# Conversions' products moved to VectorE, batch 1 masked by TensorE, batch 2 in cluster order, and a staggered order of quarter products in a fused routing-attention and PReLU-FFN kernel

## The chip, the cores and the metric

The kernel runs on one core of a Trainium2 chip. The metric is the time on the device in microseconds (us), median of three runs. Engines are named as the profile names them: PE is TensorE's matmuls and PEld its weight loads, DVE is VectorE, ACT is ScalarE, POOL is GpSimd, SP is the engine that issues most DMAs.

## What is computed

Attention over 4 batches, 8 heads, 768 tokens of 64 elements, in which a query sees only the keys that fall to the same one of 16 clusters, and behind it a feed-forward block (512 to 2048 to 512) with a leaky slope for each hidden element. The weights come as float64.

```python
q_assign = np.argmax(np.einsum('bhsd,hcd->bhsc', q_n, c_n), axis=-1)
k_assign = np.argmax(np.einsum('bhsd,hcd->bhsc', k_n, c_n), axis=-1)
mask = q_assign[:, :, :, None] == k_assign[:, :, None, :]
scores = scale * np.matmul(q, k.transpose(0, 1, 3, 2))
scores = np.where(mask, scores, -1000000000.0)
attn = softmax(scores)                 # written out in the source
x = (attn @ v).transpose(0, 2, 1, 3).reshape(B * S, H * D)
h = x @ w_in
out = (np.maximum(h, 0.0) + alpha * np.minimum(h, 0.0)) @ w_out
```

## The kernel before

**Units.** A pair `n` is one batch and two heads; there are 16 pairs, four a batch. `WHOLE = 3` batches (pairs 0 to 11, `NO = 12`) are computed against all keys: for each half of the queries (384 of them), six chunks of 128 keys for two heads. The last batch (pairs 12 to 15) is computed in cluster order: its tokens are sorted by cluster first, so that a chunk of keys meets only a window of two or three blocks of queries (L755). float32 matmuls appear in the trace as two instructions each.

**Steps.** `steps` (L747) is a list written out by hand: six steps for a pair of the whole kind (two halves of three), three for a pair in cluster order; 84 in all. Every piece of side work is put at a step and slot (`prep_at`, `load_at`, L1203 to L1247) or so many slots later (`later`, L93). Each engine executes its own instructions in the order in which the program issues them; SP's queue of DMAs too, and a DMA that waits holds all DMAs behind it on SP.

**First part** (steps 0 to 23, batch 0, the loop at L1280). The masks of batch 0 are made by TensorE: the clusters as one-hot rows (`member`, `outside`, L449 to L468; `prep_queries`, L496) go into a second, bfloat16 matmul that adds a large negative number where the clusters differ (`early_mask`, L779 and L796 to L803). The float64 weights are converted meanwhile, 32 tiles of 128 by 512 (`convert`, L241): DVE takes the words apart (`split`, L250 and L252), ACT scales (L256, L258), DVE joins (L262, L265) and POOL multiplies (L268). For the first weight matrix, four tiles make a group of quarters, from which POOL forms four sums (L305 to L313); the eight forms go to DRAM (`put`). This is an FFN by Strassen's scheme: seven products where a plain one takes eight.

**Second part** (L1321). At the first step of a half (s == 0) come the whole half's scores, in between the weighted sums (`weigh`) of the half before; then 12 slots, in which the pieces of the FFN of the batch before are fed so that they last (`feed_down_to`). Batches 1 and 2 are masked on DVE (`mask`, L822: one instruction for each chunk and head, L833, with keys from `prep_clusters`, `prep_keys`). A pair in cluster order is sorted beforehand (`order_features` to `order_scatter`): 6 stages, each of three loads on SP (L687) into one of two buffers and four scatters on POOL (L698), queued in `sorting`, of which one item is taken per slot; `order_load` fetches the sorted pair three to four steps before its start; afterwards `normalise_near`, `to_rows`, `put_back` (12 scatters on POOL, L998) and `fetch_back` bring the result back into token order.

**The FFN's hidden part** (`hidden`, L1084) makes seven products for each x, in PSUM banks a, z and b; ACT copies (five per x), DVE adds (three per x, L1077) and applies the slopes (two per x, L1081). The forms come by two loads per x into double buffers (`fetch_sums`, L1042). `final` (L1136) does the second matrix (L1147).

Of the kernel before, what the change touches and what calls it, by code (L numbers as in the profile page):

```python
# [23 lines left out]
def kernel(  # L24
# [22 lines left out]
    WHOLE = 3  # L47
# [11 lines left out]
    inp = fast.enter_context(tc.tile_pool(name="inp", bufs=4))  # L59
    vpool = fast.enter_context(tc.tile_pool(name="vpool", bufs=3))  # L60
    qkp = fast.enter_context(tc.tile_pool(name="qkp", bufs=2))
    fsp = fast.enter_context(tc.tile_pool(name="fsp", bufs=4))
# [6 lines left out]
    wsum = fast.enter_context(tc.tile_pool(name="wsum", bufs=2))  # L69
# [5 lines left out]
    memp = first_part.enter_context(tc.tile_pool(name="memp", bufs=2))  # L75
    raws = first_part.enter_context(tc.tile_pool(name="raws", bufs=1))
    cvt = first_part.enter_context(tc.tile_pool(name="cvt", bufs=3))
# [163 lines left out]
    def convert(src, dst, then):  # L241
# [6 lines left out]
        def split():  # L248
            power.append(cvt.tile([P, CW], U32, name="power"))
            nc.vector.tensor_scalar(out=power[0], in0=hi, scalar1=0x7FF00000, scalar2=None,  # L250
                                    op0=ALU.bitwise_and)
            nc.vector.tensor_scalar(out=dst.bitcast(U32), in0=hi, scalar1=0x000FFFFF,  # L252
                                    scalar2=None, op0=ALU.bitwise_and)
# [7 lines left out]
        def join():  # L261
# [6 lines left out]
            nc.gpsimd.tensor_tensor(out=dst, in0=dst, in1=power[0].bitcast(FP32),  # L268
# [23 lines left out]
    def quarters(x0, cc):  # L292
# [9 lines left out]
        def add():  # L302
# [4 lines left out]
            def summed(to, a, b, op):  # L307
                nc.gpsimd.tensor_tensor(out=forms[:, to, :], in0=forms[:, a, :],
                                        in1=forms[:, b, :], op=op)
            summed(S1, A21, A22, ALU.add)  # L310
            summed(S2, S1, A11, ALU.subtract)
            summed(S3, A11, A21, ALU.subtract)
            summed(S4, A12, S2, ALU.subtract)  # L313
# [22 lines left out]
    begun, converted = [0], [0]  # L336

    def fetch(ahead):

        while ((sources or coming) and len(fetched) < ahead  # L340
               and begun[0] + len(fetched) - converted[0] < len(raw_tiles)):
            fetched.append(convert(*next_source()))

    def advance(stages):
        stages.pop(0)()
        if stages:
            later(4 if len(stages) == 2 else 2, lambda: stages and advance(stages))
# [101 lines left out]
    def prep_argmax(n, ps):  # L449
        top, first, pieces = argmax(ps, exact=n < NCH)  # L450
# [3 lines left out]
        if n >= NCH:  # L454
# [41 lines left out]
    def prep_queries(n, half, h):  # L496
# [3 lines left out]
        if n < NCH:  # L500
# [25 lines left out]

    def second_part():

        first_part.close()
        for name, bufs in (("gpool", NQ), ("ypool", NJ), ("ppool", 2), ("emore", 1),  # L530
                           ("ordc", 1), ("ordp", 1), ("order", NP - NO), ("byrow", 1)):
            sorts[name] = fast.enter_context(tc.tile_pool(name=name, bufs=bufs))
        for i in range(4):
            e_tiles.insert(0, sorts["emore"].tile([P, 2, HS], FP32, name=f"more{i}"))

# [77 lines left out]
    def order_counts(n, ps):  # L613
# [6 lines left out]
        def scan():  # L620
            count = asg.tile([P, HS], FP32, name="simT")
# [3 lines left out]
        for i, piece in enumerate(pieces):  # L625

            later(i if i < len(pieces) - 2 else i + 2, piece) if i else piece()

# [18 lines left out]
    def order_rows(n, begin, count):  # L647
# [17 lines left out]
        later(2, lambda: order_clusters(n, begin))  # L665
# [107 lines left out]
    def score(n, half, chunks, alone=None):  # L773
# [5 lines left out]
        early_mask = n < NCH  # L779
# [42 lines left out]
    def mask(chunk):  # L822
        n, half, c, E = chunk
        if n < NCH:
# [210 lines left out]
    lagging, coming_sums = deque(), {}  # L1035
    MM, MM2 = KH * HS, DM

# [4 lines left out]
    def fetch_sums(i):  # L1042

        if i >= B * NQ:
            return
        parts = []
        for name, m0, m1 in (("early", 0, FORMS_A), ("late", FORMS_A, A21)):
            t = wsum.tile([P, m1 - m0, KH, P], FP32, name=name)
            nc.sync.dma_start(out=t, in_=by_form[i % NQ, :, m0:m1])
            parts.append(t)  # L1050
        coming_sums[i] = parts

    def ffn_pieces(b):
        rows = out[b * S:(b + 1) * S, :].rearrange(
            "(p j) n -> p j n" if b == 0 else "(j p) n -> p j n", p=P)
        gs, ys, banks, parts = {}, {}, {}, {}
# [12 lines left out]
        def product(x, k, m, rhs, start):  # L1069
            w = parts[x][m >= FORMS_A][:, m % FORMS_A]  # L1070
            for cc in range(KH):
                nc.tensor.matmul(out=bank(k), lhsT=w[:, cc, :], rhs=rhs[:, cc, :],  # L1072
                                 start=start and cc == 0, stop=cc == KH - 1,
                                 skip_group_check=not start)

# [8 lines left out]
        def hidden(x):  # L1084

            f1, f2 = x, NQ + x

            def first():
                flush()
                parts[x] = coming_sums.pop(b * NQ + x)  # L1090
                for f in (f1, f2):
                    gs[f] = sorts["gpool"].tile([P, 2, HS], FP32, name="gT")
                product(x, "a", A11, B11, True)
                nc.scalar.copy(gs[f1][:, 0, :], bank("a"))

            def second():
                product(x, "z", A12, B21, True)
                z = bank("z")
                banks.pop("z")
                lagging.append(lambda: plus(gs[f1][:, 0, :], z))  # L1100

            def third():
                product(x, "a", S2, T2, False)
                flush()
                nc.scalar.copy(gs[f1][:, 1, :], bank("a"))  # L1105

            def fourth():
                product(x, "b", S1, T1, True)
                parts["p5"] = sorts["ppool"].tile([P, HS], FP32, name="p5")
                nc.scalar.copy(parts["p5"], bank("b"))  # L1110

            def fifth():
                product(x, "a", S3, T3, False)
                nc.scalar.copy(gs[f2][:, 1, :], bank("a"))  # L1114
                p5 = parts.pop("p5")
                lagging.append(lambda: plus(gs[f2][:, 1, :], p5))

            def sixth():
                product(x, "b", S4, B22, False)
                flush()  # L1120
                end = bank("b")
                banks.pop("b")
# [500 lines left out]
```

## Time and profile before

| | |
|---|---|
| median of 3 runs | 1024.39 us (1024.2 to 1024.44) |
| the profiled execution | 1021.29 us, of it 1019.5 us span from the first to the last instruction |
| PE busy | 960.2 us, 94% of the span, 4019 matmul instructions |
| DVE busy | 692.3 us, 68% |
| ACT busy | 277.9 us, 27% |
| POOL busy | 235.5 us, 23% |
| DMA | 98.24 MB, 95 GB/s of HBM traffic over the span |
| first FFN product (L1072) | begins at 174.7 us |

A line of a window gives its length, then each engine's busy time in it with the number of instructions in brackets, in the order PE, PEld, DVE, ACT, POOL, then the granted TensorE clock (1.00 is full), the share of the DMA engines' time and GB/s. A line of the timeline gives the start, the length, the engine, the source line, the operation, what it writes and reads, the shapes, how many instructions are merged, and in brackets for how long the engine was idle before and what released it. A line of groups gives the count, the total busy time and the mean in ns of one instruction, then the engine's idle time just before.

### The profile page before, as it was taken

The numbers are of one execution on the slowest core, as the hardware profiler recorded it, in microseconds if no ns is written. First come the engines' busy times: TensorE is split into PE (matmuls) and PEld (weight loads), VectorE is DVE, ScalarE is ACT, GpSimd is POOL, SyncE is SP. The second block draws the span as 40 slices with busy tenths as digits, with TensorE's granted clock in tenths as the row PEclk, the third lists the DMA queues.
The fourth block names the chain that finished last, engine by engine and source line by source line (L and its number), as shares of the span: only waits on it lengthen the run. The fifth ranks groups of instructions, "written<-read, shape, count | busy, mean of one in ns | idle before, by whom it ended". The sixth has DMA issues, their size and how long they took to land.

```text
span 1019.5 us, 11293 instructions
## 1 busy us (share of the span) xinstructions
PE 960.2 (94%) x4019; PEld 469.4 (46%) x4019; DVE 692.3 (68%) x1178; ACT 277.9 (27%) x499; POOL 235.5 (23%) x265
## 2 busy tenths in 40 slices
PE   7976978899998899998999999999999999999997
PEld 4432433454444544444344554455445544544544
DVE  3899999987767986878878677777556624310320
ACT  4655555231232211232122331113113200201200
POOL 1464533100051323301633330000431430000000
PEclk8978988999999999998999999999999999999999
DMA  5397874362315338273520333442402322200101
GB/s 200 119 283 232 223 211 93 94 111 49 62 49 111 94 72 137 72 128 90 111 63 21 109 106 71 78 94 93 94 10 76 107 59 71 102 23 20 53 31 34
DMA packets 200544, 98.24 MB, mean 96 GB/s; under 512 B 162768, under 2 KB 182944, under 8 KB 200480
## 3 DMA queue, kind: packets, MB, share of 16 engines
q1 hardware_dynamic: 194880, 89.05, 35.4%
q0 software_dynamic: 4608, 7.87, 2.3%
q8 instruction: 34, 0.56, 0.2%
q10 hardware_dynamic: 992, 0.52, 0.2%
q14 instruction: 30, 0.25, 0.1%
HBM read 74.51 MB, written 22.54 MB: 95 GB/s over the span
## 4 chain that ended last, share of the span: by engine, by line
PE 75%; DVE 21%; issue 2%; ACT 1%; POOL 0%; ACTq 0%; DVEq 0%; POOLq 0%
PE fps L1147 30%; PE fps L1072 23%; PE fps L928 7%; PE sps L792 6%; PE fps L792 3%; DVE power L262 2%; DVE acc L843 2%; DVE more L833 2%; DVE power L250 1%; DVE forms L252 1%; DVE gT L1081 1%; DVE w_out_sb L265 1%; DVE forms L265 1%; DVE w_out_sb L252 1%; DVE gT L1077 1%
## 5 line engine op out<-in xcount | busy, mean ns | idle before, releaser
L1147 PE MATMUL fps<-w_out_sb,gT 128*128 128x512 f32 x752 | 331.5, 596 | 2.0 <-DVE gT L1081 2.0
L1147 PEld LDWEIGHTS fps<-w_out_sb,gT 128*128 128x128 f32 x752 | 140.1, 190 | 174.4 <-issue 166.0
L1072 PE MATMUL fps<-xT,early 128*128 128x384 f32 x512 | 177.6, 497 | 1.4 <-DVE gT L1077 1.0
L698 POOL DMA_INDIRECT scratch<-stage,off x96 | 101.5, 1058 | 302.9 <-DMA stage<-in_v_dram 106.3
L1072 PE MATMUL fps<-xT,late 128*128 128x384 f32 x384 | 133.1, 495 | 0.0
L1072 PEld LDWEIGHTS fps<-xT,early 128*128 128x128 f32 x512 | 96.7, 193 | 71.7 <-issue 7.7
L792 PE MATMUL sps<-qkT 64*128 64x384 f32 (+1 forms) x516 | 105.9, 532 | 4.4 <-ACT more L813 3.5
L1072 PEld LDWEIGHTS fps<-xT,late 128*128 128x128 f32 x384 | 73.8, 194 | 50.5 <-issue 3.4
L998 POOL DMA_INDIRECT back<-rows,place x48 | 47.5, 989 | 184.6 <-ACT rows L993 171.5
L1077 DVE TENSOR_TENSOR gT<-gT,fps 128x384 f32<-128x384 f32 x64 | 35.1, 548 | 68.0 <-PE fps L1072 68.0
L833 DVE SCALAR_TENSOR_TENSOR E<-aq,key,E 128x384 f32<-128x384 bf16 (+1 forms) x120 | 66.1, 606 | 18.6 <-ACT E L810 11.0
L928 PE MATMUL fps<-E,vt 128*64 128x384 f32 x384 | 75.2, 518 | 3.1 <-DVE xT L1029 3.1
L813 ACT ACTIVATE E<-sps 128x768 f32<-128x768 f32 (+1 forms) x87 | 65.4, 802 | 44.3 <-PE sps L801 37.7
L833 DVE SCALAR_TENSOR_TENSOR more<-aq,key,more 128x384 f32<-128x384 bf16 (+1 forms) x120 | 65.8, 604 | 12.8 <-ACT more L813 6.4
L792 PEld LDWEIGHTS sps<-qkT 64*128 64x128 f32 x516 | 49.4, 200 | 51.4 <-issue 16.0
L1158 DVE TENSOR_TENSOR y<-y,fps 128x512 f32<-128x512 f32 x23 | 15.8, 687 | 80.2 <-PE fps L1147 80.2
L1081 DVE SCALAR_TENSOR_TENSOR gT<-gT,alpha 128x768 f32<-128x768 f32 x64 | 62.9, 1013 | 2.2 <-ACT gT L1128 1.7
L1077 DVE TENSOR_TENSOR gT<-gT,p 128x384 f32<-128x384 f32 x32 | 17.7, 554 | 62.0 <-ACT gT L1114 62.0
L1156 ACT COPY y<-fps 128x512 f32<-128x512 f32 x24 | 14.1, 586 | 155.0 <-PE fps L1147 155.0
L928 PEld LDWEIGHTS fps<-E,vt 128*64 128x64 f32 x384 | 24.9, 142 | 42.1 <-issue 35.7
L813 ACT ACTIVATE more<-sps 128x768 f32<-128x768 f32 (+1 forms) x42 | 31.3, 795 | 43.9 <-PE sps L792 29.8
L1105 ACT COPY gT<-fps 128x384 f32<-128x384 f32 x32 | 15.3, 479 | 78.1 <-PE fps L1072 78.1
(193 smaller groups left out, 982.6 us busy)
## 6 DMA issues: line engine op xcount, KB each, us to landing
early<-sums SPq DMA_DIRECT2D x32, 512.0 KB, 3.7
late<-sums SPq DMA_DIRECT2D x32, 384.0 KB, 3.4
raw<-in_moe_w_in_dram SPq DMA_DIRECT2D x16, 512.0 KB, 6.3
sums<-forms SPq DMA_DIRECT2D x32, 256.0 KB, 4.5
raw<-in_moe_w_out_dram SPq DMA_DIRECT2D x16, 512.0 KB, 4.4
out_dram<-y SPq DMA_DIRECT2D x23, 256.0 KB, 2.1
vt<-in_v_dram SPq DMA_DIRECT2D x12, 384.0 KB, 5.4
qk<-in_q_dram SPq DMA_DIRECT2D x48, 96.0 KB, 3.8
```

Of the source, the lines that this page charges most:

```text
L252: nc.vector.tensor_scalar(out=dst.bitcast(U32), in0=hi, scalar1=0x000FFFFF, scalar2=None, op0=ALU.bitwise_and)
L262: nc.vector.scalar_tensor_tensor(out=power[0], in0=hi, scalar=0x80000000, in1=power[0], op0=ALU.bitwise_and, op1=ALU.bitwise_or)
L698: nc.gpsimd.indirect_dma_start(out=scratch[n][1][h * NX + xx], out_offset=bass.IndirectOffsetOnAxis(ap=ranks[n][:, xx, h:h + 1], axis=0), ...
L792: nc.tensor.matmul(out=bank(ps, h, m), lhsT=qkT[r:r + D, S + c * P:S + (c + 1) * P], rhs=qkT[r:r + D, tokens], start=True, stop=not early_ ...
L813: nc.scalar.activation(out=E[:, :, 0:m], in_=ps[:, :, 0:m], func=AF.Exp, scale=SCALE)
L833: nc.vector.scalar_tensor_tensor(out=e, in0=of, scalar=keys[n][:, NJ + c, h:h + 1], in1=e, op0=ALU.is_equal, op1=ALU.mult)
L928: nc.tensor.matmul(out=po[r:r + D, 0:HS], lhsT=vts[n][:, h, c, :], rhs=e[:, h, :], start=(c == 0), stop=(c == NJ - 1))
L998: nc.gpsimd.indirect_dma_start(out=to[i], out_offset=bass.IndirectOffsetOnAxis(ap=place[:, h, j:j + 1], axis=0), in_=rows[:, j, h * D:(h + ...
L1072: nc.tensor.matmul(out=bank(k), lhsT=w[:, cc, :], rhs=rhs[:, cc, :], start=start and cc == 0, stop=cc == KH - 1, skip_group_check=not start)
L1077: nc.vector.tensor_tensor(out=to, in0=to, in1=of, op=ALU.add)
L1081: nc.vector.scalar_tensor_tensor(out=g, in0=g, scalar=alpha[:, f:f + 1], in1=g, op0=ALU.mult, op1=ALU.max)
L1147: nc.tensor.matmul(out=ps[:, 0:DM], lhsT=gs[f][:, half, t * P:(t + 1) * P], rhs=w_out_sb[:, f, :], start=on and f == fs[0], stop=off and f ...
```

## The change

Five things at once, in one diff:

1. **Conversions.** The product that ends a conversion and the four sums of quarters go from POOL to DVE; the sums are spread over later slots. Only 24 of 32 conversions are done in the first part, one a step; eight come in the second part, two to each half of batch 1, with one raw buffer instead of five.
2. **Batch 1 masked by TensorE.** The conditions `n < NCH` become `n < NO`, so pairs 4 to 7 are masked by bfloat16 matmuls like batch 0, and the DVE masks, keys and query transposes of these pairs go. Rows of clusters come by DMAs on ACT's queue, as in batch 0.
3. **Batch 2 in cluster order.** `WHOLE = 2`: pairs 8 to 15 are sorted; 72 steps instead of 84. Sorting begins at steps 24, 27, 30, 33, 39, 42, 45 and 48, and two queued items are taken per slot.
4. **Quarter products.** The seven products of an x come in another order, the fourth (p4) held over into the next x; the first product is copied within PSUM by ACT so that the second accumulates onto it; DVE adds two instead of three per x. Forms are fetched one by one, eight ahead.
5. **Order at a half's start.** The weighted sum of two chunks comes before the new scores; two exp buffers fewer. The FFN of batch 1 lasts until step 66, that of batch 2 begins there, and 14 pieces of it (11 before) are kept for the time after the last step.

The diff, cut to its core:

```diff
-    WHOLE = 3
+    WHOLE = 2
-    inp = fast.enter_context(tc.tile_pool(name="inp", bufs=4))
+    inp = fast.enter_context(tc.tile_pool(name="inp", bufs=6))
-    wsum = fast.enter_context(tc.tile_pool(name="wsum", bufs=2))
+    wsum = fast.enter_context(tc.tile_pool(name="wsum", bufs=8))
...
-            nc.gpsimd.tensor_tensor(out=dst, in0=dst, in1=power[0].bitcast(FP32),
+            nc.vector.tensor_tensor(out=dst, in0=dst, in1=power[0].bitcast(FP32),
                                     op=ALU.mult)
...
             def summed(to, a, b, op):
-                nc.gpsimd.tensor_tensor(out=forms[:, to, :], in0=forms[:, a, :],
+                nc.vector.tensor_tensor(out=forms[:, to, :], in0=forms[:, a, :],
                                         in1=forms[:, b, :], op=op)
-            summed(S1, A21, A22, ALU.add)
-            summed(S2, S1, A11, ALU.subtract)
-            summed(S3, A11, A21, ALU.subtract)
-            summed(S4, A12, S2, ALU.subtract)
+            later(1, lambda: summed(S1, A21, A22, ALU.add))
+            later(1, lambda: summed(S2, S1, A11, ALU.subtract))
+            later(2, lambda: summed(S3, A11, A21, ALU.subtract))
+            later(2, lambda: summed(S4, A12, S2, ALU.subtract))
...
+    limit = [W_IN + 2 * FQ]
...
+               and begun[0] + len(fetched) < limit[0]
...
     def prep_argmax(n, ps):
-        top, first, pieces = argmax(ps, exact=n < NCH)
+        top, first, pieces = argmax(ps, exact=n < NO)
...
-        if n >= NCH:
+        if n >= NO:
             return
...
-        early_mask = n < NCH
+        early_mask = n < NO
...
     def mask(chunk):
         n, half, c, E = chunk
-        if n < NCH:
+        if n < NO:
             return
...
-        for i in range(4):
+        for i in range(2):
             e_tiles.insert(0, sorts["emore"].tile([P, 2, HS], FP32, name=f"more{i}"))
+        fast.enter_context(middle)
+        cvt[0] = middle.enter_context(tc.tile_pool(name="cvt2", bufs=1))
+        raw2 = middle.enter_context(tc.tile_pool(name="raws2", bufs=1))
+        raw_tiles[:] = [raw2.tile([P, CW, 2], U32, name="raw5")]
+        limit[0], first_ends[0] = W_IN + NF, now[0]
...
+    ORDER_OF_FORMS = (A11, S2, A12, S1, S3, S4, A22)
+    wanted = deque((b, x, m) for b in range(B) for x in range(NQ) for m in ORDER_OF_FORMS)
+    def fetch_sums(n):
+        for _ in range(n):
+            if wanted:
+                b, x, m = wanted.popleft()
+                t = wsum.tile([P, KH, P], FP32, name="form")
+                nc.sync.dma_start(out=t, in_=by_form[x, :, m])
+                coming_sums[b, x, m] = t
...
+            def product(k, m, rhs, start):
+                w = coming_sums.pop((b, x, m))
+                for cc in range(KH):
+                    nc.tensor.matmul(out=bank(k), lhsT=w[:, cc, :], rhs=rhs[:, cc, :],
+                                     start=start and cc == 0, stop=cc == KH - 1,
+                                     skip_group_check=not start)
+                fetch_sums(1)
+            def p1():
                 flush()
...
+                product(a, A11, B11, True)
+                nc.scalar.copy(bank(z), bank(a))
+                order = [p6, p2, p5] if pending else [p5, p6, p2]
+                rest.extend(order)
+                settle()
+            def p2():
+                product(z, A12, B21, False)
+                nc.scalar.copy(gs[f1][:, 0, :], bank(z))
+                banks.pop(z)
...
+            def p3():
+                product(e, S4, B22, False)
                 flush()
+                of = bank(e)
+                banks.pop(e)
+                lagging.append(lambda: plus(gs[f1][:, 1, :], of))
+                pending.append(p4)
...
-    ORDERS = [28, 34, 46, 52]
+    ORDERS = [24, 27, 30, 33, 39, 42, 45, 48]
...
-    KEPT = {B - 2: 11 * MM2 * FQ}
+    SHORT, LONG = 2 * MM2 * FQ, 14 * MM2 * FQ
+    STAGES_OF_FFN = {TOGETHER: (0, SHORT), NO * 2 * SB: (1, LONG),
+                     (NO * 2 + NCH) * SB: (None, SHORT), (NO * 2 + NCH + 2) * SB: (2, LONG),
+                     NS: None}
...
-            if u >= 0 and i < CONVERTING[u % len(CONVERTING)]:
+            if u >= 0 and i == 0:
                 convert_next()
...
             tick()
+            near = prior[1] is None
+            invert(prior[0], *((0, 1) if near else prior[1:])) if u > TOGETHER else None
+            if near:
+                weigh_near(0)
+            else:
+                weigh(GROUP, denominators=u == TOGETHER)
             if u < NS:
                 score(n, half, range(0, GROUP))
...
-            if sorting:
+            for _ in range(min(2, len(sorting))):
                 sorting.popleft()()
+            if (s, i) in ((1, 0), (2, 2)):
+                convert_next()
```

## The prediction, made before the changed kernel ran

> **What bounds the kernel now.** I read the page's slices first, then windows that cut the span at the two joints I could place in the timeline: 173 us (just before the first FFN product) and 418 us (batch 1's last half); 696 us, where the first pair in cluster order is weighed.
>
> ```profile
> PE   7976978899998899998999999999999999999997
> DVE  3899999987767986878878677777556624310320
> ```
> ```profile
> 0.00:173.00 173.00, 140.76 (x1149) 64.89 (x1149) 147.84 (x256) 93.56 (x143) 74.86 (x89) 0.88 0.70 200
> 173.00:418.00 245.00, 233.21 (x871) 109.78 (x871) 200.28 (x341) 59.82 (x114) 51.38 (x65) 0.98 0.41 86
> 418.00:696.00 278.00, 271.41 (x996) 131.98 (x992) 218.57 (x364) 69.25 (x134) 61.75 (x64) 0.99 0.38 87
> ```
>
> Two regimes. In the first 173 us PE has holes and a clock of 0.88, while DVE is full: 140.0 of the 155 us from 18 to 173. From 173 us on PE is busy 95 to 98% at a clock near 1; there only less PE work, or the 18 us of PE's waits (11.9 before 418 us, 6.5 to 696 us, all on DVE), can shorten the time.
>
> The second view is DVE and POOL side by side in the first part, where every conversion ends on POOL.
>
> ```profile
> 77.83 0.42 DVE L250 TENSOR_SCALAR power<-raw 128x512 uint32<-128x512 uint32 x1
> 78.17 0.42 DVE L252 TENSOR_SCALAR forms<-raw 128x512 uint32<-128x512 uint32 x1
> 78.50 0.69 DVE L262 SCALAR_TENSOR_TENSOR power<-raw,power 128x512 uint32<-128x512 uint32 x1
> 79.10 0.69 DVE L265 SCALAR_TENSOR_TENSOR forms<-raw,forms 128x512 f32<-128x512 uint32 x1
> ...
> 85.17 1.49 DVE L252 TENSOR_SCALAR forms<-raw 128x512 uint32<-128x512 uint32 x1
> 86.58 1.77 DVE L262 SCALAR_TENSOR_TENSOR power<-raw,power 128x512 uint32<-128x512 uint32 x1
> 88.28 1.75 DVE L265 SCALAR_TENSOR_TENSOR forms<-raw,forms 128x512 f32<-128x512 uint32 x1
> ```
> ```profile
> 86.34 6.22 POOL L308 TENSOR_TENSOR forms<-forms 128x512 f32<-128x512 f32 x4
> ```
>
> The same four instructions take 0.42, 0.42, 0.69, 0.69 us while POOL is idle, and 1.5 to 1.8 us while it adds or multiplies. So POOL does not relieve DVE here; it makes it pay.
>
> **First part: what changes.** Today's five DVE groups (L262 30.4, L250 19.5, L252 18.5 and 13.2, L265 16.3 and 14.2) sum to 112.1 us for 32 conversions, 3.50 each. Without POOL one costs 0.42 + 0.42 + 0.69 + 0.69, and the product that moves to DVE. For that I have no row of the same shape from SBUF to SBUF; L843 (two float32 SBUF inputs) takes 949 ns for 768 columns, L1077 548 for 384, so 512 lie at 0.69 us. One conversion: 2.91 us; 24 make 69.8, 16 sums of quarters 11.0, together 80.9. DVE sheds 31 us of the 140 and has 109 left after 18 us. PE is next: a step's work from back-to-back starts is 1.50 (L792), 0.42 (L801), 0.79 (L921) and 1.44 (L928), 4.15 us; 23 steps after 18 us make 95.5, features of three pairs 3 x 2.75 and four clusters' products 4 x 0.78 bring it to 107. Two engines at 107 and 109 us can't both run full in order. The steps before DVE filled up (18.12 to 44.80 us, five of them) had 24.3 us of PE work in 26.7, 91%; the bursts at each half's end (transposes, reciprocals, L1029) and the argmax stay, so I take 88%: 122 us, end at 140 instead of about 168 (the start of step 24's scores). Gain **27 us**; bounds 43 (PE never waits, end at 125) and 0 (the four DVE instructions stay at 3.50 us: 24 x 4.19 + 11 = 112, nothing shed). ACT (about 83 us after eight conversions go) and DMA (0.70 of 173 us, four MB less) fit under 122.
>
> **Batch 1.** TensorE's mask costs 0.42 us for four bfloat16 matmuls, 24 times: **+10.1 us** of PE, on the path. Their cluster rows come by four small DMAs a pair on ACT's queue; a copy or exp behind one waits with it, but the rows are made some four steps ahead and ACT is busy 60 of 245 us here. DVE loses 96 masks of 0.616 (59 us), 16 transposes L512 (9) and keys (2); it gains eight conversions (23), and the ordering of about four more pairs at 9.9 each (two L599 of 0.97 and fifteen small ones from L437 to L677, 8.0 in sum): 40. Fewer plain preparations (-7), sharper argmax (+3) and an add less per x (-4) leave about 185 us where 200 were. Eight late conversions lie in slots under FFN products, and the second matrix needs their tiles only from about step 42, some five steps after the last; without that cover they would cost PE at most their 23 us.
>
> **Batch 2.** A half's block of scores and sums against all keys, and a whole pair in cluster order:
>
> ```profile
> 226.48 1.56 PE L792 MATMUL sps<-qkT 64*128 64x384 f32 x8
> ...
> 235.12 0.85 PE L416 MATMUL mps<-qkT,cT 128*32 128x384 f32 x8
> ```
> ```profile
> 735.71 1.35 PE L792 MATMUL sps<-qkT 64*128 64x256 f32 x8
> ...
> 743.51 1.98 PE L1147 MATMUL fps<-w_out_sb,gT 128*128 128x512 f32 x4
> ```
>
> 8.64 us twice against 7.80 once: 9.48 less per pair. It pays six transposes back to rows (L990, 24 in 3.9 us: 0.98) and two beginnings (0.36 for four L633), less one L883 (0.2). Net 8.3, four pairs: **-33.3 us**. The weighed sum that now comes before the scores frees the exp buffers that are missing; between the first scores and their exp (0.81 us for a chunk) lies the next sum of 1.44 us, so I cost this at nothing. The 14 pieces kept for the end move PE work and add none.
>
> **Quarter products.** Number and size stay, so PE pays nothing if no bank is late. In the new order p6 waits for ACT's copy of p1 (0.48 us), under p4 (four instructions, 1.3 us), and p4 for one DVE add, under p3 and p1 (2.6 us). If that cover goes (DVE over 2 us late), each x stalls by the excess. Five ACT copies stay five.
>
> **Queues: the step I trust least.** Stage loads (18 a pair), single forms (224 in place of 64, about 0.34 us each on SP), the sorted pair's 12 loads and four for its return all pass SP in order, four more pairs of them, and a stage load waits until the scatters of two stages ago have landed.
>
> ```profile
> L698 POOL DMA_INDIRECT scratch<-stage,off x96 | 101.5, 1058 | 302.9 <-DMA stage<-in_v_dram 106.3 <-DVE top L674 87.2 <-DVE gT L1077 52.6
> SPq L687 <- DMA scratch<-stage,off: 48.4, 5, 28.6
> ...
> SPq L1049 <- PE fps L1072: 388.0, 56, 46.0
> ```
>
> A stage's four scatters take POOL 5.5 us (starts 286.19, 291.80, 297.17). Three loads of 0.65 on SP, 2.8 to land, 5.5, and 2.6 to land, over two buffers: 6.4 us a stage. At two items a slot and 21 us for 12 slots the program asks for one in 4.4 us, so SP falls up to 10 us behind within a half and recovers while the next half's block (10 us) runs. Seven forms ahead cover 9 us of products. At steps 51 to 61 POOL also has 12 put-backs a pair (1.29 each with the gap): about 143 us of work in 126. PE's 18 us of waits may shrink with DVE's load, and these take their place: I add **+4 us** (bounds -18, all those waits gone, and +87, rival C).
>
> The row L698 has a shortest scatter of 954 ns and a longest of 1622, beside all of DVE's present work, so a slow scatter costs 0.67 us. The Trainium skill, page "SBUF — State Buffer", section "SBUF: two separate sides" with its part "A bandwidth-pool intuition that's wrong", speaks against part of this change: while DVE runs a 2-port instruction, GpSimd can't write the descriptors of its own DMAs, and a DMA of 620 ns took 3100. The two L250/L252 instructions of each late conversion would be of that kind; if all 16 hit a scatter, 16 x 2.5 = 40 us of POOL by the page, an estimate, against 16 x 0.67 = 11 by the row. If all of it reached PE the time would be 1018 by the page and 989 by the row; the sum uses neither, since the late conversions are over by about step 37 and the pairs sorted by then start at 48.
>
> **Sum.** 1019.5 - 27 + 10.1 - 33.3 + 4 = 973.3 us of span. The profiled execution took 1021.3, 1.8 more than its span, and the median is 3.1 above that: + 4.9 = **978 us**.
>
> **Rivals.**
> - *A, the first part doesn't follow.* Raw words, forms and pairs need the DMA; from 50 to 75 us its share was 0.97. If loads, or PE's waits at half ends, hold it to a gain of 8: 997 us. Against: the mean share is 0.70 and 4 MB go.
> - *B, both parts do better.* PE reaches 94% of its time in the first part (-36) and DVE's relief takes 12 us of waits off the rest: 1024.4 - 36 + 10.1 - 33.3 - 12 = 953. For: all of those waits are on DVE.
> - *C, slower: SP's single queue starves TensorE.* Place: forms behind stage loads from step 31 to 61. 48 stages at 6.4 us each, of which SP gets none back at the blocks, cost (6.4 - 4.4) x 48 = 96; minus 9 of cover, +87: 1061. From a gain of 50 without queues, it turns the sign once 0.58 of that is lost. Against: SP waited 388 us for PE before, so it has slack, and FFN's second half needs no forms.
> - *D, nothing:* masks and sorting eat both gains. Nothing in the rows makes them equal.
>
> **How the numbers follow.** Forecast 0.62, A 0.12, B 0.17, C 0.06, D 0.03 (half of D within 0.2%, which is about what a measurement of this kernel can tell from no change; the rest split). Forecast's own range, from the first part's 20 to 35 and the queues' 0 to +15: 965 to 996. To leave out no more than two in ten I reach to B's 953 and past A: 952 to 1003. Faster 0.92, same 0.02, slower 0.06.
>
> **What would show it.** First FFN product near 147 us rather than 174.7; L250 and L265 means near 0.42 and 0.69; TensorE's clock there above 0.93. From there to batch 1's last half some 255 us, with 96 more L801. L928 from 576 to 384, L961 doubled. POOL busy near 300 us. Wrong if PE waits for a DMA form, or if the first part still ends after 160 us.

## The result, and the profile after

The changed kernel is slower: 1091.04 us (median of 4 runs, 1082.2 to 1093.58) against 1024.41 for the kernel before, timed beside it; the ratio is 1.0635, its 95% interval 1.0574 to 1.0696. The profiled execution took 1092.26 us, 1090.3 of it span. Its page, slices of PE, POOL and clock, and the shares of the chain that ended last:

```profile
PE   7998979999797997977777584999999999899997
POOL 1000010056745545464727263341302204000000
PEclk8999989999988999889979797999999999999999
PE 76%; DVE 10%; another core or an unknown queue 6%; issue 4%; ACT 2%; DMA 1%; SPq 0%; POOL 0%; ACTq 0%; DVEq 0%; POOLq 0%
```

Before, PE's slices had no hole after the first part. Now they have holes from 270 to 680 us. The two deepest slices (5 and 4 tenths, from 600 and from 654 us) come right behind slices in which POOL is busy for 7 and 6 tenths, and the clock falls there too. Windows (length, busy time of PE, PEld, DVE, ACT, POOL, then clock, DMA share, GB/s) place the loss; the joints are the first FFN product (145.3), the first scores of pair 8 (step 48) and step 60:

```profile
18.00:145.30 127.30, 119.20 (x1073) 52.43 (x1071) 110.55 (x239) 77.69 (x119) 0.55 (x2) 0.99 0.75 200
145.30:425.50 280.20, 254.72 (x942) 119.41 (x938) 182.04 (x311) 69.59 (x127) 119.20 (x138) 0.94 0.54 119
425.50:682.00 256.50, 185.42 (x634) 95.13 (x634) 129.83 (x231) 43.71 (x88) 130.83 (x147) 0.85 0.45 100
682.00:877.80 195.80, 191.08 (x666) 99.48 (x664) 109.12 (x183) 43.54 (x87) 48.05 (x48) 1.00 0.38 79
```

The first part is 29 us shorter, and PE is busy in 94% of it. Steps 48 to 60 have 185 us of PE work in 256. Inside them, the longest hole, on PE, DVE, ACT and SP (the bracket gives the idle time before):

```profile
588.87 0.82 PE L976 MATMUL fps<-E,vt 128*64 128x256 f32 x8
589.62 0.70 PE L807 MATMUL sps<-qkT 64*128 64x256 f32 x4
591.15 0.48 PE L807 MATMUL sps<-qkT 64*128 64x384 f32 x1 [0.82 <-issue]
593.24 0.48 PE L807 MATMUL sps<-qkT 64*128 64x384 f32 x1 [1.61 <-issue]
593.95 0.48 PE L807 MATMUL sps<-qkT 64*128 64x384 f32 x1 [0.23 <-issue]
596.04 0.80 PE L807 MATMUL sps<-qkT 64*128 64x384 f32 x1 [1.61 <-issue]
612.31 3.44 PE L976 MATMUL mps<-E,vt 128*64 128x384 f32 x16 [15.48 <-DVE inverses L911]
```
```profile
611.54 0.62 DVE L911 RECIPROCAL inverses<-mps 64x24 f32<-64x24 f32 x2 [31.68 <-remote]
```
```profile
610.11 0.59 ACT L1172 COPY y<-fps 128x512 f32<-128x512 f32 x1 [27.12 <-issue]
```
```profile
603.07 8.41 SPq L733 DMA_DIRECT2D qk<-scratch  x8
```

DVE's reciprocal reads sums that PE, by its records, had finished at 587.8; it starts at 611.5. ACT's copy reads products that ended at 587.7 and starts at 610.1. PE issues single matmuls 0.7 or 2.1 us apart before it stops, and SP takes 8.41 us for eight issues (5.09 for the same eight in the first run below). No operand is late: all engines stand or crawl together, and PE has no wait on a form in these steps. POOL alone keeps its pace of 1.26 us: its indirect DMAs run from 570.1 to 607.2, 29 in a row with nothing but 0.2 us copies between. I call it one run as long as the pauses in it, copies included, stay under 0.9 us. The other runs in these steps have such holes near their end too: 5 us at 429 and at 475 in runs of 12, 11 us in pieces from 539 on in a run of 28, 15 us at 655 in a run of 26. In the kernel before no run had more than 12, and none a hole of this sort.

### The profile page after: what moved, and what is told of

Read it like the earlier page. It is cut to its first block, busy times and chain, and to the rows that moved or that the text cites. A ratio compares the mean times of both kernels' runs of the same rounds, so it can differ in the third digit from the quotient of the medians.

```text
span 1090.3 us, 11926 instructions
## 1 busy us (share of the span) xinstructions
PE 965.0 (89%) x3971; PEld 478.6 (44%) x3971; DVE 586.0 (54%) x1070; ACT 265.6 (24%) x479; POOL 314.9 (29%) x385
## 4 chain that ended last, share of the span: by engine, by line
PE 76%; DVE 10%; another core or an unknown queue 6%; issue 4%; ACT 2%; DMA 1%; SPq 0%; POOL 0%; ACTq 0%; DVEq 0%; POOLq 0%
PE fps L1163 29%; PE fps L1100 24%; PE sps L807 6%; PE fps L943 5%; PE fps L807 3%; PE mps L976 2%; PE sps L816 2%; PE fps L976 1%; PE fps L936 1%; DVE acc L858 1%; PE fps L1183 1%; DVE xT L1077 1%; PE fps L392 1%; PE fps L816 1%
## 5 line engine op out<-in xcount | busy, mean ns | idle before, releaser
L1100 PE MATMUL fps<-xT,form 128*128 128x384 f32 x896 | 313.9, 509 | 45.9 <-issue 15.4
L713 POOL DMA_INDIRECT scratch<-stage,off x192 | 198.8, 1035 | 236.4 <-DMA stage<-in_v_dram 82.4
L1100 PEld LDWEIGHTS fps<-xT,form 128*128 128x128 f32 x896 | 174.6, 198 | 174.3 <-issue 35.3
L1013 POOL DMA_INDIRECT back<-rows,place x96 | 94.6, 985 | 208.5 <-ACT rows L1008 182.3
L1085 DVE TENSOR_TENSOR gT<-gT,fps 128x384 f32<-128x384 f32 x64 | 35.2, 552 | 187.7 <-PE fps L1100 158.6
L807 PEld LDWEIGHTS sps<-qkT 64*128 64x128 f32 x452 | 47.6, 196 | 42.8 <-issue 13.8
L943 PE MATMUL fps<-E,vt 128*64 128x384 f32 x320 | 61.8, 508 | 2.8 <-DVE xT L1044 2.8
L807 PE MATMUL fps<-qkT 64*128 64x384 f32 x124 | 38.6, 590 | 15.0 <-ACT E L825 14.5
L976 PE MATMUL mps<-E,vt 128*64 128x256 f32 (+2 forms) x128 | 20.2, 423 | 27.5 <-DVE inverses L911 15.5
L825 ACT ACTIVATE E<-fps 128x384 f32<-128x384 f32 x62 | 27.9, 489 | 57.3 <-PE fps L816 19.0
L848 DVE SCALAR_TENSOR_TENSOR E<-aq,key,E 128x384 f32<-128x384 bf16 (+1 forms) x64 | 33.8, 578 | 9.5 <-ACT E L825 7.9
L848 DVE SCALAR_TENSOR_TENSOR more<-aq,key,more 128x256 f32<-128x256 bf16 (+1 forms) x32 | 15.7, 545 | 34.8 <-ACT more L828 32.3
L816 PE MATMUL sps<-aq,outside 32*128 32x384 bf16 x162 | 28.0, 334 | 6.7 <-ACT outside L467 3.3
```

What stands on the lines that cost most here:

```text
L713: nc.gpsimd.indirect_dma_start(out=scratch[n][1][h * NX + xx], out_offset=bass.IndirectOffsetOnAxis(ap=ranks[n][:, xx, h:h + 1], axis=0), ...
L807: nc.tensor.matmul(out=bank(ps, h, m), lhsT=qkT[r:r + D, S + c * P:S + (c + 1) * P], rhs=qkT[r:r + D, tokens], start=True, stop=not early_ ...
L816: nc.tensor.matmul(out=bank(ps, h), lhsT=members[n][1][r, h, i * P:(i + 1) * P], rhs=aqs[n, half][r, 0, :], start=False, stop=True)
L848: nc.vector.scalar_tensor_tensor(out=e, in0=of, scalar=keys[n][:, NJ + c, h:h + 1], in1=e, op0=ALU.is_equal, op1=ALU.mult)
L943: nc.tensor.matmul(out=po[r:r + D, 0:HS], lhsT=vts[n][:, h, c, :], rhs=e[:, h, :], start=(c == 0), stop=(c == NJ - 1))
L976: nc.tensor.matmul(out=po[r:r + D, to], lhsT=vts[n][:, h, c, :], rhs=E[c][:, h, of], start=c in (1, 4), stop=c == 3)
```

## The experiments

Each run was timed beside the kernel before on the same chip. The chips turned out to differ: the kernel before has medians of 1019.5 to 1020.4 us on some (I call them **kind A**; 2, 10 and 12 in the record's numbering) and of 1023.6 to 1025.4 on others (**kind B**; 6 and 11, and by its 1024.4 the chip of the result above). Single executions of the two kinds meet at 1021. Chips 2 and 11 were used at two different times, each time with the same kind.

| run | us | before | ratio, 95% interval |
|---|---|---|---|
| e1 spaced (A) | 1162.8 | 1019.5 | 1.1421 [1.1385, 1.1457] |
| e2 bursts (A) | 1023.0 | 1019.5 | 1.0035 [1.0021, 1.005] |
| e3 batch 2 whole (A) | 1047.1 | 1019.5 | 1.0256 [1.0227, 1.0285] |
| e4 products alone (A) | 1010.8 | 1019.5 | 0.9916 [0.9899, 0.9933] |
| e5 token order (A) | 1034.9 | 1019.5 | 1.0149 [1.0126, 1.0173] |
| e6 no stage loads (A) | 998.5 | 1019.5 | 0.98 [0.9775, 0.9824] |
| e8 light space (A) | 1052.4 | 1019.5 | 1.0343 [1.0312, 1.0374] |
| e9 e3 with DVE masks (A) | 1037.4 | 1019.5 | 1.018 [1.0158, 1.0203] |
| e10 three stages (A) | 1019.2 | 1020.0 | 0.9987 [0.9968, 1.0007] |
| e11 three and space (A) | 1044.6 | 1020.0 | 1.025 [1.0225, 1.0274] |
| e12 two stages (B) | 1102.5 | 1023.6 | 1.0728 [1.0651, 1.0804] |
| e13 third from 48 (B) | 1102.1 | 1023.6 | 1.078 [1.0716, 1.0845] |
| e14 third early (B) | 1137.7 | 1023.6 | 1.1112 [1.1082, 1.1141] |
| e15 three, then four (B) | 1130.2 | 1023.6 | 1.1042 [1.1002, 1.1081] |
| e16 changed kernel again (B) | 1088.4 | 1025.4 | 1.0588 [1.0531, 1.0645] |
| e17 = e6 again (B) | 1123.3 | 1025.4 | 1.0947 [1.0919, 1.0976] |
| e18 four bursts (A) | 1019.6 | 1020.4 | 0.9996 [0.9985, 1.0007] |
| e19 changed, two bursts (B) | 1148.4 | 1025.2 | 1.1231 [1.1157, 1.1305] |

**Theories.** T1 (later T7): a long unbroken run of POOL's indirect DMAs holds up the other engines. T2: SP's single line (rival C). T3, T4: the staggered order, the masks or the late conversions. T5: the scattered rows. T6: SP's loads together with the scatters.

**e1**, small fills on POOL to break its runs:

```diff
+    def space():
+        moves[0] += 1
+        if moves[0] % 6 == 0:
+            for _ in range(32):
+                nc.gpsimd.memset(sorts["filler"], 0.0)
```

> The changed kernel, with 32 small fills on POOL after every sixth indirect DMA (about 0.11 us each by the row of L191, so some 3.5 us; 288 DMAs give 48 stretches, 168 us more of POOL). Theory T1 (a long unbroken run of indirect DMAs on POOL at 1.26 us each holds up the other engines near its end): the runs of 12 to 29 become runs of 6, the holes of PE at 475 to 480, 539 to 551, 591 to 612 and 655 to 670 us go, steps 48 to 60 take 200 us or less where they took 256, and the time falls from 1091 to 1010-1050. Theory T2 (POOL or SP is simply short of time, and forms and exp wait in its line): POOL gets 168 us more to do, so nothing falls and the time is 1090 to 1180.

A fill took 0.18 us, not 0.11, so POOL got 277 us more, and the run shows what T2 looks like. SP, then PE:

```profile
646.32 0.61 SPq L710 DMA_DIRECT2D stage<-in_v_dram  x1
665.63 0.59 SPq L710 DMA_DIRECT2D stage<-in_q_dram  x1
...
681.52 0.59 SPq L710 DMA_DIRECT2D stage<-in_q_dram  x1
...
694.86 1.58 SPq L1075 DMA_DIRECT2D form<-sums  x3
```
```profile
698.11 8.09 PE L1110 MATMUL fps<-xT,form 128*128 128x384 f32 x16 [47.60 <-DMA form<-sums]
```

SP stands from 647 to 665 and from 668 to 681 before stage loads, until POOL's scatters of two stages ago land; the forms behind them leave at 694.9, and PE waits 47.6 us (110.8 in all). So rival C exists, and it is announced by name, unlike the hole at 590. No hole like that one is in this trace; that proved nothing, for the chip is of kind A.

**e2**, bursts that nobody waits for, in the kernel before:

```diff
+        if u in BURSTS:      # {29: 12, 32: 20, 49: 28, 66: 40}
+            for i, to in enumerate(dram_disjoint_views(spare, size)):
+                nc.gpsimd.indirect_dma_start(out=to, out_offset=..., in_=sorts["before"],
+                                             in_offset=None, element_offset=i * P * P)
```

> The kernel before, with four bursts of extra indirect DMAs on POOL that nothing waits for (128 rows of 512 bytes each, to rows of their own): 12 at step 29, 20 at step 32, 28 at step 49, 40 at step 66, in stretches in which the kernel before has no scatters of its own. T1: PE stays busy beside the burst of 12, and has a hole near the end of the others, some 5 us for 20, 12 for 28, 20 or more for 40, while no operand of it is late; the time rises from 1024 to 1050-1075. T2 and all theories that blame the change's own orders: POOL's extra work has nobody waiting for it, no hole, 1024 to 1030.

3.5 us in all, and 52 in a row (with 12 of its own) without a hole but one of 2 us at its end. I took T1 for fallen. That was wrong, as e19 shows.

**e3** and **e4**, parts of the change. e3: `WHOLE = 3` in the changed kernel, four pairs sorted. e4: the two `nc.gpsimd.tensor_tensor` of L268 and L308 in the kernel before become `nc.vector.tensor_tensor`.

> The changed kernel with batch 2 whole again (masked by TensorE like batch 1), batch 3 alone in cluster order, four pairs sorted; conversions, masks, late conversions and the staggered order of products as in the changed kernel. T1: no run of POOL reaches 20, no hole above 4 us; 1024 - 14 (the first part as the changed kernel's) + 2 x 10.1 (masks of two batches) = 1030, 1022 to 1040. T3 (the staggered order or the single forms starve PE) or T4 (masks by TensorE, late conversions): the loss stays wherever FFN products run, 1060 or more.

> The kernel before with one edit: the conversions' products (L268) and the sums of quarters (L308) on DVE; all 32 conversions stay in the first part. If DVE is freed by POOL's silence as the prediction has it: 32 conversions of 2.91 us and 16 sums make 104 us where the five groups took 112, so 3 to 14 us are gained, 1010 to 1021, with L250 and L265 at 0.42 and 0.69 us. If the gain of the changed kernel's first part came from the eight conversions alone: 1022 to 1030.

Both texts count 14 us for the first part: I had taken 160.6 us for the first FFN product, which is the end of a 6 us wait inside the first ones; they begin at 145.3. Batch 2 in e3, then in the kernel before, same work but for the masks and the staggered order:

```profile
404.40:673.90 269.50, 258.39 (x970) 120.16 (x968) 131.97 (x203) 64.98 (x118) 50.83 (x59) 0.97 0.31 73
```
```profile
410.10:653.30 243.20, 236.61 (x885) 112.52 (x884) 193.02 (x322) 60.89 (x115) 64.94 (x69) 0.99 0.36 85
```

PE's busy time is 21.8 us larger (at a clock of 0.97 instead of 0.99), and the masks' own rows in it add up to 23.5: the 96 masking matmuls of a batch cost some 0.227 us each, twice what I had. The changed kernel's timeline of PE shows the four of a step:

```profile
174.20 1.56 PE L807 MATMUL sps<-qkT 64*128 64x384 f32 x8
175.69 0.82 PE L816 MATMUL sps<-aq,outside 32*128 32x384 bf16 x4
176.44 1.51 PE L943 MATMUL fps<-E,vt 128*64 128x384 f32 x8
```

From 175.69 to the next start it is 0.75 us, where the first part's row had 0.42. In the first part of the changed kernel four of them still take 0.43 (122.64 to 123.07), with L936's products behind them in place of L943's. So I took the price from a place with other neighbours; why the neighbours matter isn't shown. e4 gains 8.7 us, and its first FFN product begins at 166.1 instead of 174.7: with POOL silent the DVE instructions do shrink, but without the eight late conversions that is 8.6 us of the 29.

**e9**, e3 with batches 1 and 2 masked on DVE again (`n < NO` back to `n < NCH`); three masks of step 24 are left out, so values differ.

> The third run (batch 2 whole) with batches 1 and 2 masked on VectorE again as before, so that of the change only the conversions, the eight later ones and the staggered order are left. In that run 96 more masking matmuls a batch took PE's busy time in batch 2 from 236.6 to 258.4 us, 21.8 a batch where the prediction has 10.1. If that is the whole of its loss: 1047 - 2 x 21.8 = 1003, 995 to 1012 (before in the same job 1019.5). If the staggered order or the single forms cost PE themselves: 1015 to 1035.

PE's waits in this run name the reason:

```profile
PE fps L1100 <- DVE gT L1085: 27.4, 9, 6.5
```

The staggered order makes PE wait for DVE's add (L1085); with DVE's masks back the wait grows to 27.4 us, where e4's wait on its add (L1077) is 1.7. So the order is not free, and e3's loss is not masks alone; 1037.4 us lies above both ranges of the expectation.

**e5**, **e6**, **e8**: rows in token order, no stage loads, fewer fills (6 after every fourth DMA). e5 and e6:

```diff
-        nc.vector.tensor_scalar(out=off, in0=rank, scalar1=0.0, scalar2=float(2 * S - 1),
-                                op0=ALU.max, op1=ALU.min)
+        nc.vector.scalar_tensor_tensor(out=off, in0=rank, scalar=0.0,
+                                       in1=sorts["in_order"], op0=ALU.mult, op1=ALU.add)
...
     def order_stage(n, i):
+        if n > NO or i >= STAGES:
+            return
```

> The changed kernel with the ranks replaced by the token's own number: the same DMAs, sizes, orders and waits, but every scatter and put-back writes consecutive rows, so pairs 8 to 15 are computed in token order (other values in the output). In the changed kernel PE's semaphore came up to 24 us late and all engines but POOL stood still near the end of the runs of 12 to 29 indirect DMAs (steps 48 to 60: 256.5 us), while bursts of 12 to 40 of them to consecutive rows in the kernel before cost 3.5 us in all. T5 (it is the scattered rows of the write that do it): the holes go, steps 48 to 60 take 170-200 us, total 1010 to 1040. T6 (it is these DMAs together with SP's loads in the same stretch) and T7 (it is their number in a row, with no instruction of another kind between): unchanged, 1075 to 1100.

> The changed kernel without SP's stage loads but for the first two stages (138 of 144 loads left out; pairs 8 to 15 are made of the first pair's rows). SP then never waits for a scatter, and POOL never for a load. T6 (the loads and the scatters together): the holes go, 1010 to 1040. T2 (SP's line, the prediction's rival C): the same, since no form stands behind a stage load. T5 and T7: the holes stay, since POOL's runs get longer, 1070 to 1110.

> The changed kernel with 6 small fills on POOL after every fourth indirect DMA (in the run with 32 fills each took 0.18 us, so 1.1 us; 72 stretches, 78 us of POOL where that run had 277). The run with 32 fills had no stretch in which the other engines stood still, but waits of up to 47.6 us for a form behind a stage load. T7: the holes go without that overload, 1020 to 1060. T5, T6: they stay or POOL's extra time adds to them, 1080 to 1130.

All three ran on kind A, and none has a hole of over 2 us whose releaser isn't a named operand. e5 and e8 have waits on forms instead, 26.4 and 38.5 us; e6, with no load to stand in line, has none and takes 998.5. Steps 48 to 60 in e5, which issues the changed kernel's DMAs in its order and sizes:

```profile
413.30:625.60 212.30, 174.37 (x634) 90.65 (x632) 129.36 (x231) 43.98 (x88) 134.40 (x148) 0.93 0.53 122
```

All of e5's 26.4 us fall in this window. So on kind A rival C is what the sorting costs. What these runs say of T5 to T7 is void, since the holes they were to remove belong to kind B.

**e10**, **e11**: a third stage buffer (`STAGES = 3`) in the room that the late conversions held, all 32 conversions in the first part; e11 with e8's fills.

> The changed kernel with all 32 conversions in the first part again, and in the 6 KB a partition that this frees a third stage buffer for the sorted pairs, so that SP's stage loads wait for the scatters of three stages ago. Without stage loads the kernel took 998.5, with rows in token order 1035 with 26.4 us of PE's waits on forms. T2 (SP's line): a form stands less long behind a load, PE's waits on forms stay under 10 us; the holes in which every engine but POOL stood still are not SP's line and may stay. If both go: 1000 to 1020 (some 4 us for the eight conversions). If the holes stay: 1050 to 1095. If the waits on forms come back as the holes go: 1025 to 1050.

> The same with 6 small fills on POOL after every fourth indirect DMA, which in the run before took the holes away and left 38.5 us of PE's waits on forms (1052). If the third buffer takes those waits: 1005 to 1025. If POOL's 78 us more make the scatters late whatever the buffers: 1035 to 1060.

On kind A e10 has 5.6 us of waits on forms, and its total equals the kernel before. Its steps 48 to 60:

```profile
423.20:608.30 185.10, 167.87 (x634) 87.16 (x632) 129.18 (x231) 43.81 (x88) 126.06 (x141) 0.98 0.59 137
```

e10 differs from the changed kernel in two things, the third buffer and the early conversions, and e12, which has the early conversions alone, ran on kind B. So it isn't shown which of the two takes the waits away. The first FFN product of e10 comes at 168.0, so the eight late conversions shorten the first part by some 23 us; what they cost afterwards wasn't measured. With the fills (e11) the waits on forms are 21.3 us again.

**e12** to **e15**, on kind B: e10 with `STAGES = 2`; the changed kernel with a third buffer from step 48; with three throughout (`inp` with 5 buffers); with three, then four.

> The changed kernel with all conversions in the first part and two stage buffers as it has them, so that it differs from the run of 1019 by the third buffer alone. If the two buffers make the loss: steps 48 to 60 take 230 us or more again, 1070 to 1110. If the late conversions made it: 1015 to 1030.

> The changed kernel, late conversions kept, with a third stage buffer from step 48 on, in the 6 KB a partition that the late conversions leave. The first part then ends some 15 us earlier than in the run of 1019. If the handshake over two buffers in steps 48 to 60 is the loss: 1003 to 1020, with small holes in batch 1 (18 us in the changed kernel's trace). If the holes of batch 1 are a sign of something the buffer doesn't mend: 1030 or more.

> The changed kernel with three stage buffers from the start, the room taken from the buffers of the raw rows (five in place of six). If two buffers are the loss in batch 1 too and five raw buffers suffice: 1000 to 1012. If the sorted pairs' loads then wait for a raw buffer: 1015 to 1060.

> The same with a fourth stage buffer from step 48 on. If SP still waits for scatters in steps 48 to 60 with three: 2 to 10 us less than with three; if POOL's own time sets these steps, no less.

All four are as slow as the changed kernel or slower, whatever the buffers, and the holes are there: in e14, whose three buffers let POOL run 20 to 24 in a row before step 48 too, one of 23.1 us begins at the tenth DMA of a run of 24. So the chips came under suspicion.

**e16**, **e17**: the changed kernel and e6, unedited, again.

> The changed kernel without an edit. If the kernel before takes some 1019.5 in this call: no stretch in which all engines but POOL stand still, PE's waits on forms of 20 to 40 us (26.4 in the run in token order, 38.5 with small fills), and 1035 to 1052. If the kernel before takes 1024: 1085 to 1100 as in its first comparison. If the holes don't go with the chip: 1085 to 1100 in either case.

> The changed kernel without stage loads once more. If the kernel before takes some 1019.5: 996 to 1002 as before. If it takes 1024: should the holes need the loads and the scatters together, 1000 to 1015; should POOL's indirect DMAs to scattered rows make them alone, 1050 or more.

Both ran on one chip of kind B. Steps 48 to 60 in e6 and e17, the same code:

```profile
411.50:588.20 176.70, 165.55 (x632) 86.82 (x630) 129.31 (x231) 43.82 (x88) 123.89 (x137) 0.99 0.51 117
```
```profile
453.70:712.70 259.00, 183.79 (x632) 95.33 (x630) 129.65 (x231) 43.83 (x88) 125.48 (x144) 0.86 0.36 82
```

998.5 us on one chip, 1123.3 on another. The number of instructions is the same and the time 82 us more: PE is idle for 64 us more, and its work takes 18 us longer at the lower clock. PE's holes stand in the later half of every run of 20 to 31 or just behind it. Without stage loads POOL never waits for one and its runs get longer than the changed kernel's; on this chip e17 takes 1123.3 us where the changed kernel takes 1088.4. So T2 and T6 are out there.

**e18**, **e19**: bursts of 28, with nobody waiting, in the kernel before (to consecutive rows or to rows 28 apart, with or without fills) and in the changed kernel where its POOL is idle. The edit of e19:

```diff
+        if u in BURSTS:      # {69: False, 71: True}: consecutive rows, rows 28 apart
+            for _ in range(60 if scattered else 0):
+                nc.gpsimd.memset(filler, 0.0)
+            for i, to in enumerate(dram_disjoint_views(spare, 28)):
+                nc.gpsimd.indirect_dma_start(out=to, out_offset=..., in_=sorts["before"],
+                    in_offset=None, element_offset=i * P * (1 if scattered else P))
```

> The kernel before with four bursts of 28 indirect DMAs that nobody waits for: at step 27 to consecutive rows, at step 31 the same with 6 small fills after every fourth, at step 49 to rows 28 apart, at step 66 to rows 28 apart with the fills. On a chip where the kernel before takes 1019.5: no hole of PE by any of them, as with the bursts of 12 to 40 before. On a chip where it takes 1024: if the number in a row is enough, holes of 5 us or more in the second half of the bursts at steps 27 and 49 and none at 31 and 66; if the scattered rows are, holes at 49 and 66 alone; if both are needed, at 49 alone; if these holes need the sorted pairs' other work, none.

> The changed kernel with two bursts of 28 indirect DMAs from step 69 on, in the 160 us in which its POOL is idle: the first to consecutive rows, then 60 small fills, then one to rows 28 apart. On a chip where the kernel before takes some 1020 the bursts cost at most the 3.5 us of the second run, so the time is that of the changed kernel there: 1035 to 1052 by the runs in token order and with small fills, with PE's waits on forms of 20 to 40 us and no stretch in which all engines but POOL stand still. On a chip where it takes 1024: 1085 to 1100, and holes beside the bursts if their number in a row (both bursts) or the scattered rows (the second alone) make them; none beside them if the holes need the other work of steps 48 to 60.

e18 ran on kind A: no hole, no time. e19 ran on kind B, and there the bursts alone make the holes. The first burst joins six put-backs to a run of 34 from 771.1 to 814.3, the second one starts at 860.7 and ends, with put-backs, at 909.5. POOL around the first, then windows:

```profile
794.39 0.96 POOL L1411 DMA_INDIRECT spare<-row,number  x1 [0.30 <-issue]
...
812.06 0.96 POOL L1411 DMA_INDIRECT spare<-row,number  x1 [0.30 <-issue]
813.32 0.96 POOL L1411 DMA_INDIRECT spare<-row,number  x1 [0.30 <-issue]
847.50 0.96 POOL L1013 DMA_INDIRECT back<-rows,place  x1 [33.22 <-ACT rows L1008]
```
```profile
771.00:795.00 24.00, 23.93 (x86) 11.77 (x85) 7.31 (x11) 2.61 (x5) 18.41 (x19) 1.00 0.34 91
795.00:821.00 26.00, 5.68 (x10) 1.83 (x9) 1.17 (x3) 1.80 (x4) 14.71 (x16) 0.55 0.12 40
861.00:878.00 17.00, 17.00 (x55) 9.91 (x53) 5.79 (x7) 4.28 (x9) 13.06 (x13) 1.00 0.46 144
878.00:915.00 37.00, 12.86 (x25) 5.82 (x24) 3.15 (x4) 1.82 (x5) 24.16 (x25) 0.71 0.18 57
```

PE is full for the first 19 DMAs of the first run (13 of the second), then does 5.7 us of work in 26 (12.9 in 37), until some 6 us after the run's end. Nobody waits for the DMAs of the bursts, no stage load is under way, the DMA engines are busy for only 0.12 of the first hole, and consecutive rows do it as well as rows apart. The four executions took 1137.4 to 1157.8 us, those of the unedited changed kernel on kind B 1080.5 to 1097.4, so the 56 DMAs cost some 50 us; 44 of them stand in the two windows as time in which PE does nothing (20.3 and 24.1).

## Why the prediction was wrong, step by step

It had 973.3 us of span; measured were 1090.3, 117 more. The step that failed is the +4 us for the queues, below.

- **First part: right, in part by luck.** First FFN product near 147, measured 145.3; L250 and L265 at 411 and 684 ns; clock 0.99; DVE's busy time after 18 us 110.6 against 109. DVE's term holds. The two terms of PE missed against each other, and that the end came out right is luck: 119.2 us of work where I had 107, at 94% of the time instead of 88. Rival A falls.
- **Masks: right in kind, half in size.** 10.1 us predicted, 21.8 for a batch by e3.
- **Batch 2 in cluster order.** From the first scores of pair 8 to the end, e6 (no loads, kind A) takes 584.2 us (411.5 to 995.7), the kernel before 609.4 (410.1 to 1019.5): some 25 gained where I had 33.3. Where no queue is in the way this step holds roughly.
- **Quarter products: the cover I named was not there.** Costed at nothing; PE waits 14.9 us for L1085's adds (17 to 20 in e5, e6 and e8), 6.0 of them in the first products of batch 1, at 154.6 us, while DVE is at work on sums and a conversion.
- **Queues: the step that failed.** "These take their place: I add +4 us." I priced POOL's line by who waits for what it delivers. The runs show on kind B a price of another sort: during a long run of indirect DMAs PE, DVE, ACT and SP stop, whoever waits for them. Steps 48 to 60 took 256.5 us, where on kind A they took 185.1 in e10 and 176.7 in e6: 71 to 80 us. Batch 1 up to pair 8's scores took 280.2, in e6 265.9: 14 more. Together 85 to 94 of the 117; the masks' 11.7, the 8 us that batch 2 gained less, and the adds make most of the rest. e6 and e10 aren't the changed kernel; the one pair with the same code on both kinds, e6 and e17, gives 82 us in these steps. On kind A the +4 would have been too small as well, by SP's line: e5 takes 212.3 us there, 36 more than e6, 26.4 of them waits on forms.
- **Rival C had the place but not the mechanism.** In the whole trace of the changed kernel PE waits for no form, and the first part ended at 145.3 us: both signs that I had named for being wrong stayed away (in e16 PE waits 5.8 us for one form). On kind A, in neighbours of the change, this wait is the cost that decides (26.4 us in e5, 38.5 in e8, 110.8 in e1; 5.6 in e10).
- **The skill's rule.** The prediction weighed the Trainium skill, "SBUF — State Buffer", section "SBUF: two separate sides": while DVE runs an instruction in a 2-port mode, GpSimd can't write the descriptors of its DMAs. The trace doesn't show it as a cost: POOL's instructions for the scatters (L713) take 1035 ns on average, 1058 before, and the six indirect DMAs that ran beside an L250 or L252 took 1057, the longest of them 1263. What decided is the reverse, POOL's DMAs stopping the others.

Not measured: the unedited changed kernel on kind A; fills against the holes on kind B; e4 on kind B. What differs between the chips, and what in the run stops the engines, stays open; so does whether a pause on POOL would prevent it. On kind A e4 is the one kernel with the reference's full computation that is faster than the kernel before (1010.8 us against 1019.5).

## What to carry to other kernels

Count how many indirect DMAs stand in a row on POOL, not only whether somebody waits for them: on kind B runs of 12 cost 0 to 8 us of PE's time here, and runs of 26 to 38 some 13 to 24 us each. Whether pauses between them help isn't shown: in e12 a hole of 11.5 us begins beside the second of two runs of 8 that lie 1 us apart. A hole in which several engines idle with "issue", "remote" or an unknown queue as releaser, and no late operand, wasn't mended by buffers here (e13 to e15); look at what the one busy engine does. And before an experiment clears a theory, run the unedited kernel on the same chip: ten runs here were blind to the effect they were to remove or to make.

## What the hardware showed that I had not expected

- On kind B, after 8 to 22 indirect DMAs at 1.26 us each with no pause of 0.9 us or more, PE, DVE, ACT and SP crawl or stop (the eighth in e13 at 297 us, the 22nd in the changed kernel at 539). They recover between 2 us before and 7 us after the run's end. During the hole POOL keeps 0.96 + 0.30 us a DMA. On kind A 52 to 58 in a row (e2, e6, e10) did nothing of it.
- A hole costs twice: the granted clock was 0.55 from 795 to 821 us in e19, and 0.85 as a mean over steps 48 to 60 of the changed kernel, against 0.98 to 0.99 in e10 and e6; PE's work in these steps took 185.4 us there and 165.6 in e6.
- The kernel before differs by 0.5% between the kinds (1019.5 and 1025), the changed one without loads by 12.5% (998.5 and 1123.3).
